# A bucketed attention and expert kernel: a reordered start, pairs 0 and 1 hashed singly, loads behind a gate

## The chip, the cores and the metric

The kernel runs on one core of a Trainium2 chip. The metric is the device time of one execution in microseconds (us). The median of three runs of the kernel before is 390.04 us (389.36 to 390.91).

The engines are TensorE (PE; PEld is its weight load), VectorE (DVE), ScalarE (ACT), GpSimd (POOL) and SyncE (SP). SP and ACT also issue DMAs from their queues.

## What is computed

Attention over 4 batches of 8 heads, 768 tokens, 64 columns, in which a query sees only the keys of its own hash bucket; then one expert layer on the 128 best scored tokens of each batch.

```python
q_bits = (q @ proj > 0); k_bits = (k @ proj > 0)          # 6 bits
mask = bucket(q_bits)[:, None] == bucket(k_bits)[None, :]
scores = where(mask, scale * q @ k.T, -1e9)
attn = softmax(scores) ; o = attn @ v
# per batch: x = o of all heads (768 x 512)
s = x @ w_gate ; top = 128 largest of s
h = max(x[top] @ w1, 0) ; y = h @ w2
out = x ; out[top] += sigmoid(s[top]) * y
```

## The kernel before, in words

Every value that matters is split into a high 16-bit part and a low remainder, so that PE multiplies 16-bit numbers. Heads come in pairs: pair p holds heads 2p+1 and 2p+2 in the two halves of the 128 partitions; head 0 is loaded apart (`init_first`, `load_first`), its operands are split on ACT (`split_first`, `split_second`) and DVE (`low_first`).

For a pair, `load_x` brings the 384 KB of its queries (r = 0) and of its keys (r = 1) on SP's queue. `split_xh` makes the high part in tile T on ACT, `split_xl` the low part on DVE. `k_diff` subtracts the two halves of the keys' high part (GpSimd for pair 0, DVE after). The hash multiplies X by the six projections as 32-bit matmuls into a PSUM bank: `hash_half(g, e)` takes half e of the tokens of the two pairs 2g and 2g+1 together. `signs(g, e)` compares the result with zero on DVE into tile sg and, after the second half, subtracts the two halves of the signs (GpSimd for group 0, DVE after). Head h's operand A is then put together in SBUF by DMAs on SP's queue: `place_a` (the high parts), `place_signs` (the bits, two DMAs), `place_b` and `place_l` (the operands of the low-part product).

For every head, six pairs of matmuls (`max_unit`) give each query's bucket scores; `max_relu` (ACT) and `max_red` (DVE) reduce them to a maximum per query. `max_turn`, `max_copy` and `max_row` turn the maxima into a row of A; head 0 does this in two steps by `row_first` (PE and a copy by ACT). Then come the scores (`st_unit`, two matmuls, `st_exp` on ACT), the remainder of the exponentials (`r_chunk`, DVE or GpSimd), and the product with V (`av`). V's 384 KB are loaded by `load_v` on ACT's queue and split by `split_vh` (ACT) and `split_vl` (DVE). `sum_v` to `seed` prepare what the product starts from. `norm` divides.

The PSUM banks for maxima, hash and rows are four, handed out in a fixed turn (`pmax.take`, `pmax.give`). The expert weights come through `load_w`, one resumption of the generator `weights` at a time.

The order in which instructions are issued is written out by hand: `at` numbers the events and the tuple `ORDER` lists them; a negative number resumes a generator (weights, the choice of tokens, the experts, the last batch's `rank_last`). Every engine runs its own instructions in this order. `mine` remembers the last marked DVE instruction, and `turn` makes a GpSimd instruction wait for it. In the start, `keep_warm` puts matmuls on PE whose result is not used.

At the end, `rank_last` ranks the last batch's tokens: `compare` on DVE counts for each token how many come before it, `count` adds the rest by matmuls with a column of ones, and `pick` makes the selection matrix from rank and position, which 48 matmuls (L1177) then multiply.

Of the kernel before, what the change touches and what calls it, by code (L numbers as in the profile page):

```python
# [12 lines left out]
F16 = mybir.dt.float16  # L13
# [37 lines left out]
TURNS = True  # L51
PJW = 69
# [1315 lines left out]
```

## Time and profile before

| | us |
|---|---|
| median of 3 runs | 390.04 |
| the profiled execution | 389.61 |
| its span, first to last instruction | 387.5 |
| PE busy | 374.8 (97%) |
| DVE busy | 345.9 (89%) |
| ACT busy | 313.3 (81%) |
| GpSimd busy | 181.2 (47%) |

Busy time is an engine's time in instructions; matmuls are pipelined and their ends are modelled, so a busy PE is not a PE at its peak. The granted clock is the share of 2.4 GHz that PE was given. Instructions appear with line, engine, operation, the tile written and those read, partitions x elements.

### The profile page before, as it was taken

To read this page: it belongs to the slowest core of one execution; us is meant where nothing else is said; L and a number is where in the kernel's file an instruction comes from. 1 tells how busy PE (TensorE), PEld (TensorE's weight loads), DVE (VectorE), ACT (ScalarE), POOL (GpSimd) and SP (SyncE) were. 2 spreads that over 40 slices of the span, in tenths; PEclk is the share of its full clock that TensorE was granted. 3 is DMA by queue.
4 is the path that set the end of the run, shared out by engine and by line. 5 is a ranking of instruction groups with operands and counts; after the bars stand their busy time and mean duration, and the time that the engine had idled before them with its cause. 6 is when DMAs were issued, how large, how long until landed. Compare 5 with 4: busy or idle time off the path is not lost.

```text
span 387.5 us, 14129 instructions
## 1 busy us (share of the span) xinstructions
PE 374.8 (97%) x5728; PEld 272.6 (70%) x5738; DVE 345.9 (89%) x935; ACT 313.3 (81%) x665; POOL 181.2 (47%) x103
## 2 busy tenths in 40 slices
PE   6889999999999999999999999999999999999995
PEld 4346777677676777687657877667677788778794
DVE  3889999999899989999999999999999999999842
ACT  7899999899998988988588888988988995774210
POOL 8135567474647275655335362545236352630113
PEclk9799999999999999999999999999999999999999
DMA  7568677677776475565855552756463524010301
GB/s 243 148 193 232 172 199 232 169 203 177 223 209 181 100 214 125 140 188 150 208 136 157 135 155 61 217 161 177 100 178 103 113 58 125 6 38 3 110 29 56
DMA packets 26353, 56.37 MB, mean 145 GB/s; under 512 B 4218, under 2 KB 10942, under 8 KB 26288
## 3 DMA queue, kind: packets, MB, share of 16 engines
q1 hardware_dynamic: 15936, 36.92, 36.6%
q10 hardware_dynamic: 9680, 16.45, 13.5%
q0 software_dynamic: 672, 2.10, 1.7%
q8 instruction: 45, 0.74, 0.8%
q14 instruction: 20, 0.16, 0.2%
HBM read 26.58 MB, written 7.35 MB: 88 GB/s over the span
## 4 chain that ended last, share of the span: by engine, by line
PE 78%; issue 7%; ACT 5%; DVE 5%; DMA 2%; POOL 1%; POOLq 0%; SPq 0%; ACTq 0%; DVEq 0%
PE av L776 24%; PE bank L671 14%; PE st L722 14%; PE st L726 14%; PE bank L463 3%; PE bank L995 3%; PE bank L1019 2%; DMA A<-sg 2%; DVE R L757 2%; ACT me L679 1%; ACT P L740 1%; DMA Xa<-in_qk_dram 1%; DVE mj L688 1%; DVE jks L813 1%; PE bank L598 1%
## 5 line engine op out<-in xcount | busy, mean ns | idle before, releaser
L760 POOL TENSOR_TENSOR R<-P 128x1536 f16<-128x1536 f32 x46 | 133.8, 2910 | 134.4 <-DVE V L556 21.1
L776 PEld LDWEIGHTS <-P 128*128 128x128 bf16 x2304 | 125.8, 98 | 26.7 <-issue 1.3
L776 PE MATMUL av<-V,P 128*128 128x65 f16 (+2 forms) x2304 | 133.3, 193 | 0.1
L776 PE MATMUL av<-V,R 128*128 128x65 f16 (+1 forms) x1152 | 126.4, 193 | 0.0
L740 ACT ACTIVATE P<-st 128x512 f32<-128x512 f32 x192 | 111.9, 598 | 17.7 <-PE av L776 9.7
L722 PE MATMUL st<-A 128*128 128x512 f16 (+1 forms) x384 | 119.3, 326 | 1.4 <-ACT P L740 1.2
L726 PE MATMUL st<-B 128*128 128x512 f16 (+1 forms) x384 | 118.6, 326 | 0.7 <-ACT B L432 0.7
L688 DVE CUSTOM_DVE_ANT_0 mj<-bank,me 128x384 bf16<-128x384 f32 x192 | 102.2, 550 | 15.6 <-ACT me L679 7.4
L671 PE MATMUL bank<-A 128*128 128x384 f16 x384 | 108.4, 329 | 3.8 <-DVE A L410 1.0
L776 PEld LDWEIGHTS <-R 128*128 128x128 f16 x1152 | 105.9, 97 | 0.1
L679 ACT ACTIVATE me<-bank 128x384 f32<-128x384 f32 x192 | 92.4, 491 | 14.8 <-PE bank L671 5.7
L757 DVE TENSOR_TENSOR R<-P 128x768 f16<-128x768 f32 x100 | 96.8, 987 | 0.4 <-ACT P L740 0.2
L742 ACT ACTIVATE P<-st 128x512 f32<-128x512 f32 x96 | 56.9, 596 | 2.2 <-PE st L726 0.7
L671 PEld LDWEIGHTS <-A 128*128 128x128 f16 x384 | 34.8, 98 | 23.1 <-issue 4.8
L726 PEld LDWEIGHTS <-B 128*128 128x128 f16 x384 | 37.5, 98 | 18.0 <-issue 2.5
L722 PEld LDWEIGHTS <-A 128*128 128x128 f16 x384 | 37.4, 97 | 15.8 <-issue 2.5
L502 DVE SCALAR_TENSOR_TENSOR T<-X,T 128x768 f16<-128x768 f32 x32 | 31.4, 992 | 0.0
L495 ACT ACTIVATE T<-X 128x768 f16<-128x768 f32 x32 | 26.6, 841 | 0.4 <-DMA B<-T 0.4
L837 POOL TENSOR_TENSOR w1l<-W,w1h 128x512 bf16<-128x512 f32 x8 | 12.8, 1604 | 13.6 <-DVE M L688 4.9
L837 POOL TENSOR_TENSOR w2l<-W,w2h 128x512 bf16<-128x512 f32 x8 | 12.3, 1545 | 12.5 <-DVE R L757 4.0
L798 DVE TENSOR_TENSOR x<-av,rc 128x384 f32<-128x384 f32 x32 | 17.7, 553 | 0.2
L995 PEld LDWEIGHTS <-w1h 128*128 128x128 f16 x256 | 15.9, 98 | 2.1
(137 smaller groups left out, 409.5 us busy)
## 6 DMA issues: line engine op xcount, KB each, us to landing
X<-in_qk_dram SPq DMA_DIRECT2D x32, 384.0 KB
B<-T SPq DMA_DIRECT2D x62, 192.0 KB
A<-T SPq DMA_DIRECT2D x31, 240.0 KB
V<-in_v_dram ACTq DMA_DIRECT2D x16, 384.0 KB
out_dram<-x ACTq DMA_DIRECT2D x6, 768.0 KB
W<-in_w_dram ACTq DMA_DIRECT2D x8, 512.0 KB
sbc<-scores SPq DMA_DIRECT2D x3, 384.0 KB
A<-sg SPq DMA_DIRECT2D x31, 31.5 KB
```

Of the source, the lines that this page charges most:

```text
L502: mine(nc.vector.scalar_tensor_tensor(t[:, o : o + S], st["X", p, r], XS, t[:, i : i + S], op0=ALU.mult, op1=ALU.subtract))
L671: nc.tensor.matmul(pt[:, :384], a[0][:, t * P : (t + 1) * P], a[1][:, 384:768] if i else K[h % NA], start=True, stop=True,)
L679: nc.scalar.activation(me, st["mx", h, t, 0][:, :384], AF.Relu)
L688: nc.vector.tensor_tensor_reduce(out=jk, in0=st["mx", h, t, 1][:, :384], in1=st["me", h, t], op0=ALU.add, op1=ALU.max, scale=1.0 / MS, sca ...
L722: nc.tensor.matmul(pt[:, o : o + n], a[1][:, c * P : (c + 1) * P], a[0][:, q0 : q0 + n], start=True, stop=False,)
L726: nc.tensor.matmul(pt[:, o : o + n], bt[:, 0, c * P : (c + 1) * P], bt[:, 1, q0 : q0 + n], start=False, stop=True,)
L740: nc.scalar.activation(pp[:, r, 0:512], pt, AF.Exp, scale=ES)
L742: nc.scalar.activation(pp[:, :, 512:768], pt.rearrange("p (a b) -> p a b", a=2), AF.Exp, scale=ES)
L757: mine(nc.vector.tensor_tensor(t[:, r], pp[:, r], hi_view(pp, r), op=ALU.subtract))
L760: turn(nc.gpsimd.tensor_tensor(t, pp, hi_view(pp, a), op=ALU.subtract))
L776: nc.tensor.matmul(o[:, t, :n], l, vv[:, c, hh, v0 : v0 + n], start=False, stop=last and l is lo, skip_group_check=True,)
L995: nc.tensor.matmul(hp[:, f * P : (f + 1) * P], w[:, k, o : o + P], x[:, k * P : (k + 1) * P], start=(f == 0 and k == 0 and i == order[0]), ...
```

## The change

- *Loads.* Of the constants only the identity is loaded early (`load_ident`); the rest of the constants, pair 1's X and V of pair 0 wait for the last of head 0's sign compares on DVE (`gate`). V of pair 0 is issued on SP's queue and no more on ACT's. The issue of V of pair 1 and of the first expert weight stands, on ACT, behind the first two maxima of head 1.
- *Hash.* Pairs 0 and 1 are hashed one at a time, all tokens together (`hash_pair`, `sign_pair`): per pair 64 partitions, two compares, one subtraction, all on DVE.
- *High parts.* `split_xh(0, 1)` and `split_xh(1, 0)` run on GpSimd.
- *Identity.* Its 16-bit copy is made by DVE.
- *The last rank.* A 32-bit matmul with the identity (`behind`) starts the bank of counts with each token's constant, so that the selection compares with the rank alone.
- One score instruction of batch 1 (`HOLD`) becomes a mark for `turn`.
- *Order.* The first 300 or so events are reordered; after that 11 events move by a few places. After `begin` the old order read: `load_x(0,1)`, `load_x(1,0)`, `load_x(1,1)`, four signs of head 0, ..., `load_x(0,0)`, two `max_relu`, ..., `load_first(0)`, ..., `load_v(0)`, `load_consts`, `split_xh(1,0)`, `(1,1)`, `(0,0)`, `make_ident`, ..., `hash_half(0,0)`, `(0,1)`, ..., `k_diff`, `place_a(1)`, ..., `signs(0,0)`, `(0,1)`, ..., `place_signs(1)`, ..., `row_first(1)`, `max_unit(1,4,0)`. The new one reads:

```
load_first(0), sign_first(0,0), init_rest, init_a(1), load_x(0,1), split_xh(0,1), sign_first(1,0),
sign_first(1,1), diff_first, max_unit(0,1,1), max_unit(0,0,0), split_second(0), load_x(0,0),
low_first(0), sign_first(0,1), load_ident, make_ident, max_unit(0,0,1), init_m, max_relu(0,0),
max_red(0,0), max_unit(0,1,0), hash_pair(0), max_relu(0,1), split_xh(0,0), max_red(0,1),
max_unit(0,2,0), max_unit(0,3,0), sign_pair(0), max_unit(0,2,1), load_first(1), split_second(1),
max_relu(0,2), max_relu(0,3), max_unit(0,3,1), max_red(0,2), k_diff(0), load_v(0), max_unit(0,4,0),
max_red(0,3), load_x(1,1), split_vh(0), split_vl(0), load_x(1,0), max_relu(0,4), max_unit(0,5,0),
max_relu(0,5), max_unit(0,4,1), place_a(1), row_first(0), max_unit(0,5,1), sum_v(0), load_consts,
max_red(0,4), split_xh(1,1), st_unit(0,3), st_exp(0,3), max_red(0,5), init_a(2), row_first(1),
st_unit(0,4), sum_hi(0), place_signs(1), max_unit(1,0,0), st_exp(0,4), max_unit(1,4,0),
max_relu(1,0), hash_pair(1), split_xl(0,1), max_relu(1,4), weights(1), split_xl(0,0), load_v(1), ...
```

`keep_warm(2)` and `keep_warm(3)`, eight matmuls each, stand before among head 0's maxima, after in head 1's maxima and in head 2's scores.

```diff
+HOLD = ((1, 1, 4),)
+    def load_ident():
+        nc.sync.dma_start(cs[:, :P], cst[:, :P])
+
     def load_consts():
-        nc.sync.dma_start(cs, cst)
+        behind_of(nc.sync.dma_start(cs[:, P:], cst[:, P:]), "gate", "load")
     def make_ident():
-        nc.scalar.copy(ident16, ident)
+        nc.vector.tensor_copy(ident16, ident)
+    def behind_of(i, key, why):
+        if key in st:
+            tc.add_manual_dep(
+                getattr(i, "ins", i), getattr(st[key], "ins", st[key]).name,
+                mybir.DependencyInfo(mybir.DependencyClass.Sync, mybir.DependencyReason.SCHED_ONLY),
+                reason=why,
+            )
     def load_x(p, r):
-        nc.sync.dma_start(x, qk[p, r])
+        i = nc.sync.dma_start(x, qk[p, r])
+        if p == 1:
+            behind_of(i, "gate", "load")
     def load_v(pr):
-        (nc.scalar if ACT_V else nc.sync).dma_start(t, v[pr])
+        i = (nc.scalar if pr else nc.sync).dma_start(t, v[pr])
+        if not pr:
+            behind_of(i, "gate", "load")
...
         if r:
-            nc.vector.tensor_scalar(
+            st["gate"] = nc.vector.tensor_scalar(
...
+    def hash_pair(p):
+        hp = st["hpp", p] = pmax.take(f"hpp{p}")
+        for e in range(2):
+            for r in range(2):
+                i = 64 * e + 32 * r
+                nc.tensor.matmul(
+                    hp[i : i + 32, :384], pjt[:, 0:32], st["X", p, r][:, e * 384 : (e + 1) * 384],
+                    start=True, stop=True, tile_position=(0, i),
+                )
+
+    def sign_pair(p):
...
+        w = slice(64 * p, 64 * p + 64)
+        hp, t = st["hpp", p], st["sg", 0][w]
+        sd, sg = t[:, : S // 2], t[:, S // 2 :]
+        for e in range(2):
+            i = slice(64 * e, 64 * e + 64)
+            nc.vector.tensor_scalar(
+                sg[:, e * 384 : (e + 1) * 384], hp[i, :384], pjt[i, 66:67], pjt[i, 67:68],
+                op0=ALU.is_gt, op1=ALU.mult,
+            )
+        pmax.give(f"hpp{p}")
+        mine(nc.vector.tensor_tensor(sd, sg[:, 0:384], sg[:, 384:768], op=ALU.subtract))
     def split_xh(p, r):
-        nc.scalar.activation(st["T", p][:, o : o + S], st["X", p, r], AF.Copy, scale=XS)
+        if (p, r) not in {(0,1),(1,0)}:
+            nc.scalar.activation(st["T", p][:, o : o + S], st["X", p, r], AF.Copy, scale=XS)
+        else:
+            nc.gpsimd.tensor_scalar(st["T", p][:, o : o + S], st["X", p, r], XS, None, op0=ALU.mult)
+            if (b, part, t) in HOLD:
+                mine(i)
+    def behind(rp):
+        nc.tensor.matmul(
+            rp[:, :NC], ident, cs[:, 3 * P + NC : 3 * P + 2 * NC], start=True, stop=False, skip_group_check=True
+        )
...
         for t in range(NC):
-            pick(sel, t, rank)
+            nc.vector.tensor_scalar(sel[:, t], iota16, rank[:, t : t + 1], None, op0=ALU.is_equal)
```

## Rows read from the trace of the kernel before

**Rows 1.** The page: busy us (share of span) and instructions of each engine.
```profile
PE 374.8 (97%) x5728; PEld 272.6 (70%) x5738; DVE 345.9 (89%) x935; ACT 313.3 (81%) x665; POOL 181.2 (47%) x103
```

**Rows 2.** Windows: length, busy PE, PEld, DVE, ACT, POOL, granted clock, DMA share, GB/s.
```profile
5.00:10.00 5.00, 3.32 (x23) 1.31 (x23) 2.99 (x5) 4.62 (x8) 4.63 (x18) 0.79 1.03 342
10.00:15.00 5.00, 5.00 (x33) 1.92 (x32) 3.67 (x11) 4.10 (x8) 0.44 (x1) 0.53 0.59 149
15.00:20.00 5.00, 3.57 (x25) 1.56 (x23) 5.00 (x10) 4.39 (x9) 0.91 (x1) 1.00 0.54 152
20.00:25.00 5.00, 3.96 (x34) 2.12 (x32) 4.07 (x14) 4.47 (x11) 2.04 (x1) 1.00 0.96 279
25.00:30.00 5.00, 4.73 (x68) 2.99 (x57) 4.67 (x13) 5.00 (x13) 1.98 (x3) 1.00 0.40 86
```

**Rows 3.** Timeline, 10 to 20.1 us: start, length, engine, line, operation, count [idle before <-releaser].
```profile
10.29 0.35 ACTq L383 DMA_DIRECT2D V<-in_v_dram  x1
...
10.69 2.31 ACT L495 ACTIVATE T<-X 128x768 f16<-128x768 f32 x3
...
11.42 2.78 PE L463 MATMUL bank<-X,pjt 128*32 128x384 f32 x16
...
12.90 0.28 ACT L348 CAST ident<-cs 128x128 f16<-128x128 f32 x1
...
13.31 0.67 DVE L480 TENSOR_SCALAR sg<-bank,pjt 128x384 f16<-128x384 f32 x1
...
15.03 0.91 POOL L489 TENSOR_TENSOR sg<-sg 128x384 f16<-128x384 f16 x1 [4.59 <-DVE sg L480]
...
15.97 1.77 SPq L509 DMA_DIRECT2D A<-sg  x2
...
19.14 0.65 PE L671 MATMUL bank<-A 128*128 128x384 f16 x3 [0.22 <-DMA A<-sg]
19.44 0.34 ACT L454 CAST A<-bank 1x256 f16<-1x256 f32 x1
...
20.05 0.33 PE L671 MATMUL bank<-A 128*128 128x384 f16 x1
```

**Rows 4.** Timeline, 5 to 9 us: head 0's signs and the first X copy.
```profile
5.76 0.57 ACT L415 ACTIVATE s<-bank,pjt 14x384 f32<-14x384 f32 x1
...
5.91 1.39 DVE L410 TENSOR_SCALAR A<-bank,pjt 14x384 f16<-14x384 f32 x2
6.36 0.61 ACT L416 ACTIVATE A<-s,pjt 14x384 f16<-14x384 f32 x1
...
8.12 0.83 ACT L495 ACTIVATE T<-X 128x768 f16<-128x768 f32 x1
```

**Rows 5.** Groups by form, 0 to 36 us: count | busy us, mean ns.
```profile
L679 ACT ACTIVATE me<-bank 128x384 f32<-128x384 f32 x21 | 9.8, 491 | 1.8 <-PE bank L671 0.6 <-PE st L726 0.5 <-DVE M L688 0.4
...
L661 DVE TENSOR_TENSOR T<-T 128x384 f16<-128x384 f16 x2 | 0.8, 378 | 0.0
```

**Rows 6.** Groups by form, 0 to 36 us: GpSimd's memsets and the weights' remainder.
```profile
L321 POOL MEMSET A<- 32x960 f32 x7 | 6.3, 897 | 2.0 <-PE st L722 1.8
...
L837 POOL TENSOR_TENSOR w1l<-W,w1h 128x512 bf16<-128x512 f32 x2 | 2.8, 1406 | 3.0 <-DVE R L757 1.8 <-DMA A<-sg 1.2
```

**Rows 7.** Timeline, 4 to 16 us: head 0's two low parts on DVE.
```profile
4.92 0.95 DVE L438 SCALAR_TENSOR_TENSOR B<-Xa,A 64x768 f16<-64x768 f32 x1 [3.02 <-ACT A L392]
...
15.34 1.41 DVE L438 SCALAR_TENSOR_TENSOR B<-Xa,B 64x768 f16<-64x768 f32 x1
```

**Rows 8.** Timeline, 361 to 372 us: the last rank and selection.
```profile
361.67 1.56 PE L1143 MATMUL bp<-cs,sc 128*128 128x128 f32 x12
...
367.89 1.43 DVE L874 TENSOR_SCALAR sel<-iota,cs,rank 128x128 f16<-128x128 f16 x6
...
368.79 2.84 PE L1177 MATMUL bank<-sel,xs 128*128 128x128 f16 x48
```

**Rows 9.** Timeline of PE, 39 to 42 us: the second group's hash.
```profile
39.83 1.50 PE L463 MATMUL bank<-X,pjt 128*32 128x384 f32 x16
```

More of the change, by code (lines that the diff above doesn't have):

```diff
@@ L360, in mine @@
         st["port"] = i
-    def turn(i):
-        if TURNS and "port" in st:
-            tc.add_manual_dep(
-                getattr(i, "ins", i), getattr(st["port"], "ins", st["port"]).name,
-                mybir.DependencyInfo(mybir.DependencyClass.Sync, mybir.DependencyReason.SCHED_ONLY),
-                reason="port",
-            )
+    def behind_of(i, key, why):
[5 more added lines that the diff above has]
+            )
+    def turn(i):
+        if TURNS:
+            behind_of(i, "port", "port")
     def need(*keys):
@@ L456, in row_first @@
         st[("row1", 0) if e else ("row", 0)] = True
+    def hash_pair(p):
[8 more added lines that the diff above has]
+    def sign_pair(p):
+        if ("sg", 0) not in st:
+            st["sg", 0] = sb.tile([P, S // 2 + S], F16, tag="sg", name="sg0", bufs=2)
+        w = slice(64 * p, 64 * p + 64)
[7 more added lines that the diff above has]
+            )
+            st["sgd", p, e] = True
+        pmax.give(f"hpp{p}")
+        mine(nc.vector.tensor_tensor(sd, sg[:, 0:384], sg[:, 384:768], op=ALU.subtract))
     def hash_half(g, e):
@@ L485, in signs @@
         if e:
-            if g:
-                mine(nc.vector.tensor_tensor(sd, sg[:, 0:384], sg[:, 384:768], op=ALU.subtract))
-            else:
-                nc.gpsimd.tensor_tensor(sd, sg[:, 0:384], sg[:, 384:768], op=ALU.subtract)
+            mine(nc.vector.tensor_tensor(sd, sg[:, 0:384], sg[:, 384:768], op=ALU.subtract))
     def split_xh(p, r):
@@ L812, in score @@
             jk = sb.tile([P, 384], BF16, tag="jks", name=f"jks{b}_{part}_{t}", bufs=2)
-            nc.vector.tensor_tensor_reduce(
+            i = nc.vector.tensor_tensor_reduce(
                 out=jk[:, : d1 - d0], in0=x[:, t, d0:d1], in1=wgt[:, d0:d1],
@@ L862, in compare, with count @@
         ))
-    def count(i, cm, rp):
+    def behind(rp):
+        nc.tensor.matmul(
+            rp[:, :NC], ident, cs[:, 3 * P + NC : 3 * P + 2 * NC], start=True, stop=False, skip_group_check=True
+        )
+    def count(i, cm, rp, first=True):
         for j in range(i, NC):
             nc.tensor.matmul(
-                rp[:, j : j + 1], cm[:, j], oneb[:, 0:1], start=(i == j == NC - 1), stop=(i == 0),
+                rp[:, j : j + 1], cm[:, j], oneb[:, 0:1], start=first and i == j == NC - 1, stop=(i == 0),
                 skip_group_check=True,
@@ L1153, in rank_last @@
         rp = st_bank(f"rp{b}")
+        behind(rp)
         yield
@@ L1161, in rank_last @@
             if i < NC - 1:
-                count(i + 1, cms[i + 1], rp)
+                count(i + 1, cms[i + 1], rp, False)
                 yield
-        count(0, cms[0], rp)
+        count(0, cms[0], rp, False)
         yield
@@ L1242, in body @@
         at(keep_warm, 2 + i, n)
-    for g in range(NH // 4):
+    for p in range(2):
+        at(hash_pair, p)
+        at(sign_pair, p)
+    for g in range(1, NH // 4):
         for e in range(2):
@@ L1246, in body @@
             at(signs, g, e)
+    at(load_ident)
     for fn in (score_v, score_vh, score_vl):
```

308 rows, old and new, of the table ORDER are left out of this document.

## The prediction

> **What bounds the kernel now.** I read three views, in this order. The page's busy shares come first: TensorE (PE) is busy 97% of the span [rows 1], and a busy PE is not a PE at its peak. So a gain must come from a place where PE waits or runs slowly. The windows of the first 30 us show one [rows 2]: from 5 to 10 us PE works 3.32 of 5 us, from 10 to 15 us it is busy all the time but at a granted 0.53 of the clock (mostly the lower level, 1.2 GHz), from 15 to 25 us it works 7.53 of 10. From 25 us on PE (4.73), ACT (5.00) and DVE (4.67) are full together. The start is a chain of small steps, not a rate: head 0's bits and maxima, its row of maxima, then head 1's operands. The timeline of the start is the third view, and what the reader should look for there is what stands in these queues that this chain does not need. There is much of it. ACT makes three copies of X in one stretch of 2.31 us between two maxima; PE runs the hash of pairs 0 and 1 together for 2.78 us; only then can DVE compare (0.67 each), GpSimd subtract (0.91) and SP send head 1's bits (1.77 us of issue), and head 1's first maxima start at 19.14 with that DMA as their releaser [rows 3]. Head 0's second row of maxima is copied at 19.44, ending at 19.78 [rows 3]. These two times, 19.14 and 19.78, are my milestones.
>
> **The change part by part.** Head 0's bits are as before: the same two ACT steps of 0.57 and 0.61 per half and two DVE compares in 1.39, ending at 7.30 [rows 4].
>
> *ACT up to the second row copy.* After the change ACT has, from 5.76 on: four sign steps 2.36; two copies of the second operand, one X copy (0,0), one V copy and the X copy (1,1), each about 0.77 (a third of the 2.31 in [rows 3]; widths are 768 columns), 3.85; six maxima of 0.49 [rows 5], 2.94; the row copies 0.56 (estimate: 512 columns by the 0.34 for 256 in [rows 3] and the 0.49 for 384 in [rows 5]) and 0.34; one exponential, about 0.6 (same estimate). The sum is 10.65, so the row is done at 5.76 + 10.65 = 16.4 if ACT never waits, against 19.78: 3.4 us earlier. What has left the stretch: X copies (0,1) and (1,0), now GpSimd's, and (2,1), put later, 2.3 together; the identity's cast 0.28 and the issue of V's load 0.35 [rows 3]; the rest are waits for maxima that come late.
>
> *Head 1's bits.* The first pair is now hashed alone, behind head 0's first maximum. That maximum is read by ACT at about 9.4 (two signs, a copy, two signs, one maximum after 5.76), which frees the bank. The hash of one pair is half of 2.78 at the same clock, 1.39, so 10.8; two compares of 0.67 [rows 3], 12.2; the subtraction, now on DVE, 0.38 [rows 5], 12.6; the two issues 1.77, 14.4; landing as before 1.4 us behind the issue (19.14 - 15.97 - 1.77), 15.8. Against 19.14 that is 3.3 us earlier. Both milestones move alike, by about 3.3.
>
> *GpSimd's new copies.* No row shows this operation. Bounds: a memset of 960 columns takes 897 ns and a two-input subtraction of 512 columns 1406 ns [rows 6], so 768 columns cost between 0.7 and 2.1 us. I take 1.3, nearer to the memset since one tensor is read, not two. It costs nothing: pair 0's half is on GpSimd once X has landed (before 8.12, when ACT's first copy of it ran [rows 4]), ends by 10.2 even at 2.1, k's subtraction of 0.91 by 11.1, and head 1's large operand goes out about then, ahead of the bits at 12.6. Were this cover gone, the milestone would slip by what exceeds about 1.5 us.
>
> *What DVE takes on.* Two more compares of 0.67 (64 partitions cost as much as 128), two subtractions of 0.38 (one from GpSimd, one because pairs are single), the identity's cast about 0.2: 2.3 us. DVE works 6.66 of the 10 us from 5 to 15 [rows 2], so 3.3 us of idleness hide it; without that cover it would cost up to 2.3.
>
> *A shared port.* One DVE step with two tensors took 0.95 beside a memset and 1.41 beside GpSimd's subtraction [rows 7], 0.46 more. The Trainium skill, "GPSIMD Engine Reference", section 1, says GpSimd shares its SBUF interfaces with VectorE and contends with instructions that have two SBUF inputs; that speaks against more work on GpSimd here, the rows agree, and by it three such steps would cost 1.4 us, 388.6 us in all if nothing covered them. I take zero in the sum, since DVE has the idleness named above.
>
> *Loads behind the gate.* The waits for the last compare at 7.3 stand in SP's queue. Behind them on SP are only V's first load, pair 1's X, the rest of the constants and head 1's operands, none of which is wanted before about 11. V's load moves from ACT's queue to SP's. The gain of the gate itself, a quicker first X, I put at zero; what it may cost is a rival.
>
> *How much survives.* From about event 330 the order is the same as before except for single swaps, so what is gained when PE, ACT and DVE become full stays. The lower bound is what ACT is rid of for good: two copies 1.54, cast 0.28, issue 0.35, 2.2 us. The upper bound is the milestones' 3.3. I take 3.0, nearer to the milestones, because what bounds the rest is PE, which gains the earlier start and not ACT's relief.
>
> *The tail.* The rank's seed adds one 32-bit matmul of 6 columns with its weights. Six of 128 columns took 1.56 us [rows 8], so at most 0.26, at least 0 (in the shade of a DVE wait); I take 0.15, since PE runs without a pause there. The six selections in 1.43 us become simpler, but the 48 matmuls that read them start only after the expert's matmuls and then run at 59 ns each (2.84 / 48) [rows 8], so a faster selection is worth 0. The one new port mark of batch 1's score and the single swaps in the middle: 0, with 0.3 either way.
>
> The sum: -3.0 + 0.15 = -2.85. The profiled execution took 389.61 (span 387.5 and 2.1 around it), 0.43 under the median of 390.04; it becomes 386.76, and the median **387.2**.
>
> **The rivals.** *PE stays at half clock (1.2 GHz).* Before, the granted clock is 0.79, 0.53 and then 1.00 (2.4 GHz) in the three stretches from 5 to 20 us: it rose after one in which PE was busy 5.00 of 5 with the joint hash, maxima and warm-up matmuls [rows 2]. The same 16 hash matmuls take 2.78 at half clock and 1.50 at full [rows 3, 9]. The change takes the dense stretch away: the hash is halved and 16 warm-up matmuls go far behind. The Trainium skill, "TensorE: Matmul & The Clock Gate", Part 1, says the throttled state is the default and activity releases it; by that rule sparser matmuls may delay the release, and the windows bear it out. The price from rows: doubling PE's work from 15 to 20 us needs 3.57 more where 1.43 is idle, 2.1 net; from 20 to 25, 3.96 less 1.04, 2.9; from 25 to 30, 4.73 less 0.27, 4.5 [rows 2]. Busy time overlaps (three maxima in 0.65, one alone 0.33 [rows 3]), so I count six tenths. Half clock to 18 us costs 0.8: **388.0**. *The same, long:* half clock to 28 us costs 0.6 x (2.1 + 2.9 + 2.7) = 4.6, **391.8**, which is slower than before; it decides from about 24 us on, where it eats the 2.85. Against it: at half clock PE becomes the full engine by 15 us, and being full is what preceded the rise.
>
> *Gated loads come late.* Three loads of 0.39 MB start at 7.3. At the 342 GB/s of 5 to 10 us they land by about 12, at the 150 of 10 to 20 us [rows 2] by about 16.5; then pair 1's hash and head 2's bits slip 1 to 2 us. Taking 1.5: **388.7**. For it: the place of pair 1's X behind V. Against: 150 was demand and not capacity.
>
> *Nothing carries on.* The early gain is eaten by the work put off (the X copy of pair 2, DVE's 2.3 us) where ACT and DVE are full, or the gates order nothing that was late: **390.0**.
>
> **How the numbers follow.** The forecast 0.60, the short half clock 0.15, late loads 0.12, nothing 0.06, the long half clock 0.07. The range of the forecast alone: 3.3 and another 0.7 for the spread of the runs (389.36 to 390.91) on the low side, 385.6; 2.2 with 0.3 for the swaps on the high side, 388.5. Of the other cases the short half clock, late loads with their 2 us and a little more belong inside, so the high end is 389.6; outside stay nothing, the long half clock and parts of the others, under 0.2. About 0.5% (1.95 us) is what a measurement can tell from no change. Faster by more: 0.56 of the forecast's 0.60, 0.07 of the short half clock, 0.03 of late loads, 0.66. Slower by more: only the long half clock and mishaps with it, 0.07. Between: 0.27.
>
> **What would show it.** Right: head 0's second row copy near 16.4 instead of 19.78, head 1's first maxima near 15.8 instead of 19.14, and from there every stage about 3 us earlier to the end. GpSimd's copies between 0.7 and 2.1 us with nobody waiting for them. Wrong: a granted clock near 0.5 beyond 15 us; head 1's maxima released by pair 1's or by GpSimd's work; DVE full before 15 us; a shift that is there at 16 us and gone at 50; or a first X that lands no earlier and a hash that waits for it.

## The result and the profile after

The changed kernel takes 392.84 us in the median of five runs (390.39 to 394.08) against 390.04 of before: a ratio of 1.0058, 95% interval 1.0035 to 1.0081. The forecast was 387.2, between 385.6 and 389.6. The profiled execution took 391.89, its span is 389.9, 2.4 more than before's 387.5. TensorE's share of the span is as before (97%), VectorE's busy time is 5.4 us longer [rows 1], 2.6 of it in one blocked step that is shown below. Busy us, share and instructions on the page of the kernel after:

```profile
PE 377.6 (97%) x5740; PEld 273.1 (70%) x5740; DVE 351.3 (90%) x940; ACT 313.0 (80%) x662; POOL 183.8 (47%) x104
```

The windows of the first 30 us answer to [rows 2]: length, busy time of PE, PEld, DVE, ACT and POOL, granted clock, DMA share, GB/s.

```profile
5.00:10.00 5.00, 3.24 (x24) 1.09 (x20) 4.61 (x9) 4.77 (x9) 3.30 (x5) 0.77 0.87 296
10.00:15.00 5.00, 4.48 (x32) 1.54 (x24) 4.53 (x13) 4.29 (x8) 4.76 (x6) 0.50 0.65 204
15.00:20.00 5.00, 5.00 (x40) 2.18 (x31) 4.15 (x10) 3.75 (x10) 1.64 (x1) 0.71 0.65 122
20.00:25.00 5.00, 4.98 (x33) 2.71 (x32) 4.64 (x16) 4.96 (x13) 2.21 (x1) 1.00 1.03 317
25.00:30.00 5.00, 4.84 (x83) 3.73 (x82) 5.00 (x14) 4.99 (x11) 1.88 (x2) 1.00 0.81 219
```

The granted clock is 0.71 from 15 to 20 us, where before had 1.00: TensorE stayed at 1.2 GHz until 17.9 us. The timeline of the start answers to [rows 3] (GpSimd's two copies, the issue of head 1's bits, head 0's second row copy, head 1's first maxima on TensorE and ScalarE):

```profile
7.01 2.19 POOL L533 TENSOR_SCALAR T<-X 128x768 f16<-128x768 f32 x1 [1.64 <-DMA X<-in_qk_dram]
...
12.72 1.77 SPq L547 DMA_DIRECT2D A<-sg  x2
...
14.24 2.40 POOL L533 TENSOR_SCALAR T<-X 128x768 f16<-128x768 f32 x1
...
16.77 0.34 ACT L466 CAST A<-bank 1x256 f16<-1x256 f32 x1
...
17.10 0.85 PE L709 MATMUL bank<-A 128*128 128x384 f16 x2
...
17.84 0.49 ACT L717 ACTIVATE me<-bank 128x384 f32<-128x384 f32 x1
```

The row copy ends at 17.1 instead of 19.78, and head 1's first maxima start on TensorE at 17.10 instead of 19.14 [rows 3]. So the start did come earlier, by 2.0 to 2.7 us. To follow what becomes of it, one small DVE step per head serves as a milestone: the add ahead of a head's reciprocal (L787 before, L825 after). In before those of heads 1, 23 and 24 (counted from 0) are

```profile
48.80 0.17 DVE L787 TENSOR_TENSOR rc<-av,rc 128x6 f32<-128x6 f32 x1
...
278.66 0.17 DVE L787 TENSOR_TENSOR rc<-av,rc 128x6 f32<-128x6 f32 x1
...
288.15 0.16 DVE L787 TENSOR_TENSOR rc<-av,rc 128x6 f32<-128x6 f32 x1
```

and in after

```profile
48.52 0.17 DVE L825 TENSOR_TENSOR rc<-av,rc 128x6 f32<-128x6 f32 x1
...
278.35 0.17 DVE L825 TENSOR_TENSOR rc<-av,rc 128x6 f32<-128x6 f32 x1
...
290.19 0.16 DVE L825 TENSOR_TENSOR rc<-av,rc 128x6 f32<-128x6 f32 x1
```

Read down: of the early start 0.28 us is left at head 1 and 0.31 at head 23; one head later the kernel is 2.04 behind. There are two losses, one between 18 and 48 us and one between 278 and 290.

The second is one instruction. In before, the last of batch 2's score steps (jks, 0.48 each) started 0.59 us ahead of GpSimd's remainder R:

```profile
286.58 0.48 DVE L813 CUSTOM_DVE_ANT_0 jks<-x,wgt,sc 128x256 bf16<-128x256 f32 x1
...
286.99 0.55 DVE L688 CUSTOM_DVE_ANT_0 mj<-bank,me 128x384 bf16<-128x384 f32 x1
287.17 2.75 POOL L760 TENSOR_TENSOR R<-P 128x1536 f16<-128x1536 f32 x1 [5.71 <-ACT P L740]
```

In after, one reduction of maxima (mj) stands ahead of the score steps instead of behind them, and they come later against R:

```profile
285.34 0.55 DVE L726 CUSTOM_DVE_ANT_0 mj<-bank,me 128x384 bf16<-128x384 f32 x1
...
286.63 3.05 DVE L851 CUSTOM_DVE_ANT_0 jks<-x,wgt,sc 128x256 bf16<-128x256 f32 x1
286.65 2.75 POOL L798 TENSOR_TENSOR R<-P 128x1536 f16<-128x1536 f32 x1 [5.50 <-ACT P L778]
...
290.14 0.32 PE L709 MATMUL bank<-A 128*128 128x384 f16 x1 [1.71 <-DVE W L655]
...
291.12 0.49 ACT L717 ACTIVATE me<-bank 128x384 f32<-128x384 f32 x1 [2.48 <-DVE M L726]
```

The score step takes 3.05 us instead of 0.48: it waits for R's whole 2.75. TensorE then stands 1.71 us and ScalarE 2.48 for what VectorE owes them.

### The profile page after: what moved, and what is told of

Its sections match the earlier page's. It is cut to its first block, busy times and chain, and to the rows that moved or that the text cites. A ratio compares the mean times of both kernels' runs of the same rounds, so it can differ in the third digit from the quotient of the medians.

```text
span 389.9 us, 14156 instructions
## 1 busy us (share of the span) xinstructions
PE 377.6 (97%) x5740; PEld 273.1 (70%) x5740; DVE 351.3 (90%) x940; ACT 313.0 (80%) x662; POOL 183.8 (47%) x104
## 4 chain that ended last, share of the span: by engine, by line
PE 76%; DVE 8%; issue 6%; ACT 4%; DMA 3%; POOL 1%; SPq 0%; POOLq 0%; DVEq 0%; ACTq 0%
PE av L814 23%; PE bank L709 15%; PE st L760 14%; PE st L764 14%; PE bank L1040 3%; DMA A<-sg 3%; DVE R L795 2%; DVE jks L851 2%; PE bank L1064 2%; PE bank L501 2%; ACT P L778 1%; ACT me L717 1%; DVE mj L726 1%; DMA Xa<-in_qk_dram 1%; PE bank L636 1%
## 5 line engine op out<-in xcount | busy, mean ns | idle before, releaser
L726 DVE CUSTOM_DVE_ANT_0 mj<-bank,me 128x384 bf16<-128x384 f32 x192 | 102.4, 551 | 10.3 <-PE bank L709 4.8
L709 PEld LDWEIGHTS <-A 128*128 128x128 f16 x384 | 35.2, 98 | 24.5 <-issue 7.0
L531 ACT ACTIVATE T<-X 128x768 f16<-128x768 f32 x30 | 25.1, 841 | 0.4 <-DMA B<-T 0.4
L877 POOL TENSOR_TENSOR w1l<-W,w1h 128x512 bf16<-128x512 f32 x8 | 11.7, 1467 | 18.8 <-DVE T L699 6.5
```

The source lines that it names most:

```text
L709: nc.tensor.matmul(pt[:, :384], a[0][:, t * P : (t + 1) * P], a[1][:, 384:768] if i else K[h % NA], start=True, stop=True,)
L726: nc.vector.tensor_tensor_reduce(out=jk, in0=st["mx", h, t, 1][:, :384], in1=st["me", h, t], op0=ALU.add, op1=ALU.max, scale=1.0 / MS, sca ...
```

## The experiments

Ratios are to before on the same chip, with 95% intervals; where microseconds are worked out from two ratios of different batches, they are 390 times the difference. The order is given by the names of the events; in the code ORDER holds their numbers.

**First question: the collision, the front or the tail?** Three theories stood against each other: that the collision is the whole loss, that the new front is slower by itself, and that the tail's added matmul costs. e1 undoes the one swap at batch 2's score:

```diff
+ choose2 (scores 3 to 5 of batch 2's second part)
  max_red(27, 2)
- choose2
```

> The changed kernel with one step put back: the second step of choose(2) (three scores on DVE) stands again ahead of the reduction max_red(27,2), as before. Theory A (collision): of the loss, 2.2 us come from one score on DVE that took 3.05 us instead of 0.42 at 286.63, because GpSimd's remainder began at 286.65; with the old order DVE is then in a reduction that reads PSUM, the score keeps its 0.42, and the time is 2 to 2.5 us under the changed kernel's 392.84, about 390.4. Theory B (the new front is slower by itself and this place only shows it): another wait takes over, 392 to 393. Theory C (the end of the kernel, with its added matmul): no change, 392 to 393.

Measured: 390.27 us, 1.0017 (1.0006 to 1.0027). In its profile R starts 0.50 behind the last score step, which takes 0.48. By the ratios that is 1.6 us better than after.

e2 leaves the order and marks the step, so that GpSimd waits for it:

```diff
- HOLD = ((1, 1, 4),)
+ HOLD = ((1, 1, 4), (2, 1, 5))
```

> The changed kernel with its order, but the last score of that step (batch 2, part 1, column 5) gets the mark that GpSimd's remainder waits for. Theory A: GpSimd starts about 0.4 us later, behind the score, the score takes 0.42 us, and the time is about 390.4 as in e1_swap_back, 0.2 more at most. Theories B and C: 392 to 393.

Measured: 390.74, 1.0020 (1.0008 to 1.0032); batch 2's three score steps take 0.47 each, and R starts 0.65 behind the last. Two different cures give the same 1.5 to 1.6 us, and both intervals lie under after's (1.0035 to 1.0081): the collision is shown. Both kernels are still not faster than before, so it isn't all.

e3 takes the front alone (after's first 300 events and their code, before's order behind them, no mark, no seeded rank); e4 takes the rest alone.

```diff
  # e3
- ORDER = after
+ ORDER = after[:300] + before[299:]
- HOLD = ((1, 1, 4),)
+ HOLD = ()
```

> The new front alone (loads, single hashes, GpSimd copies, the first 300 events); the order behind it, the scores' marks and the last rank are those of before. Theory A: 0.1 to 0.6 us under before (the shift of head 23's reciprocal in the profiles was 0.4), 389.5 to 390. Theory B: 2 to 3 us over before, 392 to 393. Theory C: as before, 390.

Measured: 389.40, 0.9985 (0.9969 to 1.0002), and a second time, as e3_again:

> The new front with the rest of before, a second time, as the base of the next three runs. It gave 389.40 beside 389.89 of before. Expected 389.2 to 389.7 beside a before of 389.9. Its profiled front ran at the lower clock to 19.4 us; if that end moves from run to run, the theory of the clock (below) expects the times of this kernel to spread by over 1.5 us, as they did the first time (387.96 to 390.70).

Measured: 389.57, 0.9991 (0.9976 to 1.0006), between 388.22 and 391.58. The front is worth about 0.5 us of the 3.0 forecast, and both intervals still hold no gain at all.

> The other half: the front of before with everything behind the first 300 events as in the changed kernel (swaps, the score's mark, the last rank). Theory A: the swapped score meets GpSimd's remainder here too, 2 to 2.8 us over before, 392 to 393. Theory B: as before, 390. Theory C: 392 to 393, but with the loss behind 360 us and not at 286.

Measured: 390.99, 1.0024 (1.0013 to 1.0034): 0.9 us lost. Its profile doesn't show the collision although it has the swap: the last score step has a lead of 0.11 us on R, keeps its 0.48, and R takes 2.97 instead of 2.75. In after the lead is 0.02 and the score step loses. Leads of 0.07 to 0.17 stand in ten other profiles (0.11 in before itself, at batch 1's score), and the score step keeps its 0.48 or 0.49 in all of them. The swap turned a lead of 0.59 into 0.11 and 0.02 in these two profiles; that some executions of after escape, which would explain their wide spread, is argued from this and not shown.

**Second question: where do 2 us of the front go?** Three cures on e3. f1 puts the two groups of eight warm-up matmuls back among head 0's maxima, f2 issues head 3's bits where SyncE's queue is empty, f3 does both.

```diff
  # f1                              # f2
  max_unit(0, 0, 1)                 load_x(3, 1)
+ keep_warm(3, 8)                 + place_signs(3)
  ...                               ...
  max_unit(0, 2, 1)                 max_row(1)
+ keep_warm(2, 8)                   ...
  ...                             - place_signs(3)
- keep_warm(2, 8)   (at 23 us in e3_again)
  ...
- keep_warm(3, 8)   (at 43 us in e3_again)
```

> The kernel e3 with the two groups of eight warm-up matmuls put back among head 0's maxima, one behind its second and one behind its sixth product, where TensorE waits for a bank. Theory 'clock': the front lost its gain because TensorE stays at 1.2 GHz to 17.7 to 19.4 us instead of 14.7; then the clock is full by about 15 us here, the reciprocal of heads 2 to 5 comes 0.5 to 1.5 us earlier than in e3, and the time is about 388.6. Theory 'head 3's bits' and theory 'full engines' (what the front gains has to be given back where TensorE, ScalarE and VectorE are all full): within 0.3 us of e3, whatever the clock does.

> The kernel e3 with the two transfers of head 3's bits issued right behind the load of pair 3's second operand, where SyncE's queue stands empty for 5 us, instead of behind head 1's row of maxima. Theory 'head 3's bits': in after and in e3 these transfers are the last thing that head 3's first maxima wait for (issued 27.7, landed 32.5 in after; in before issued 21.3); then the first maxima of head 3 come 2 us earlier than in e3, the reciprocal of heads 2 to 5 0.8 to 2 us earlier, and the time is about 388.2. Theories 'clock' and 'full engines': head 3's first maxima move, the reciprocals do not, and the time is within 0.3 us of e3.

> Both changes on e3. If clock and bits are two separate losses, the gains of the two add up, about 387.6, faster than before by 0.5%. If the front's gain must be given back to full engines, 389.1 to 389.7 as e3.

Measured: f1 389.15, 0.9976 (0.9964 to 0.9987); f2 389.14, 0.9969 (0.9954 to 0.9983); f3 388.56, 0.9959 (0.9946 to 0.9973). A second time, as f3_again:

> f3 a second time, as the base of the next run and because it is the fastest kernel so far. It gave 0.9959 of before; expected 0.995 to 0.997, 388.3 to 389.0 beside a before of 390.0.

Measured: 388.44, 0.9969 (0.9954 to 0.9984). Against e3_again, on the same chip, f1 is 0.6 us faster, f2 0.9 and f3 1.2; the intervals of f1 and f2 overlap with e3_again's, that of f3's first run just clears it. f3 beats before by 1.2 to 1.6 us and after by 3.5 to 3.9. But the theories failed in their detail. In f1 and f3 the clock is full from 11.4 and 5.6 us on, and head 1's first maximum comes at 18.55 and 18.03, no earlier than in e3_again (18.02). The other profiles say the same: it comes at 17.4 to 18.7 in the ten with a full clock from 13.7 us or earlier, and at 17.8 to 19.0 in the six with half clock to 17.5 us or later. The clock isn't what holds it. In f3 (issue of the bits, TensorE's first maxima of head 1):

```profile
13.00 1.77 SPq L547 DMA_DIRECT2D A<-sg  x2
...
17.67 0.48 PE L709 MATMUL bank<-A 128*128 128x384 f16 x2 [1.02 <-DMA A<-sg]
```

the maxima wait for head 1's bits, 4.67 us after the issue began; in before it was 3.17 (19.14 less 15.97 [rows 3]). And head 3's first maxima come no earlier in f2 than in e3_again (33.42 and 33.26 on ScalarE); what moved is the second reciprocal.

What the cures do is seen in one window, from head 1's first maximum on ScalarE to the second reciprocal's add: length, busy time of PE, PEld, DVE, ACT, POOL, clock, DMA share, GB/s. Before:

```profile
19.91:48.80 28.89, 27.50 (x383) 18.28 (x382) 26.10 (x71) 28.01 (x63) 15.24 (x8) 1.00 0.72 199
```

After:

```profile
17.84:48.52 30.68, 29.64 (x397) 19.64 (x397) 28.39 (x73) 28.15 (x62) 13.88 (x8) 1.00 0.73 200
```

The window is 1.79 us longer: TensorE has 2.14 us more to do in it and stands 0.35 less. The early start was partly bought by putting work behind the milestone: pair 1's hash (0.85), sixteen warm-up matmuls, and for VectorE two compares, a subtraction and a low part (2.3). One profile is not much here: the same window is 28.86 to 28.89 us in all four kernels with before's front (before, e4, h2, h3), but 30.28 to 31.47 in the five with after's (after, e1, e2, e3 twice). That it is longer with the new front is sure, how much is not. e3_again and the cured kernels f1, f2 and f3 in this order:

```profile
18.02:49.11 31.09, 29.43 (x396) 19.45 (x389) 28.50 (x73) 28.01 (x62) 13.87 (x8) 1.00 0.69 199
```

```profile
18.55:49.24 30.69, 28.98 (x381) 18.70 (x381) 28.84 (x75) 27.99 (x61) 13.62 (x8) 1.00 0.70 198
```

```profile
18.17:48.43 30.26, 29.62 (x397) 19.63 (x397) 28.47 (x74) 28.30 (x62) 13.88 (x8) 1.00 0.72 208
```

```profile
18.03:47.92 29.89, 28.97 (x381) 18.77 (x381) 28.27 (x74) 28.08 (x61) 13.82 (x8) 1.00 0.71 207
```

Against e3_again f1 has 0.45 us less work for TensorE and a window 0.40 shorter, which is within that spread; in f2 TensorE's idleness falls from 1.66 to 0.64 and the window by 0.83, to just under the spread; f3's is 1.20 shorter, and f3_again's (29.90) agrees.

A window is TensorE's work and its idleness together, whatever the cause; more is learned from where the idleness stands. With after's front much of it stands in one place, ahead of head 2's scores. Before (the copy of head 2's row of maxima, and head 2's first scores):

```profile
34.24 0.25 ACT L703 CAST mr<-bank 6x128 f16<-6x128 f32 x1 [0.22 <-PE bank L698]
...
38.28 0.38 PE L722 MATMUL st<-A 128*128 128x512 f16 x1
```

After:

```profile
35.03 0.24 ACT L741 CAST mr<-bank 6x128 f16<-6x128 f32 x1
...
38.54 0.39 PE L760 MATMUL st<-A 128*128 128x512 f16 x1 [0.67 <-ACT T L531]
```

These scores in e3_again, then in f3:

```profile
39.13 0.39 PE L760 MATMUL st<-A 128*128 128x512 f16 x1 [1.50 <-DMA A<-mr]
```

```profile
37.99 0.39 PE L760 MATMUL st<-A 128*128 128x512 f16 x1 [0.26 <-DMA A<-mr]
```

In after head 0's first scores start 1.47 us earlier than in before (15.20 for 16.67) and head 1's 1.21 earlier (28.48 for 29.69), but head 2's row of maxima is copied 0.79 later, and its scores start 0.26 later. The early start is lost there. TensorE doesn't wait in before; with after's front it waits 0.34 to 1.60 us, for the transfer of the row in four of the five profiles; in f2 0.41, in f3 0.26. What is shorter in f2 and f3 is that transfer: its issue starts at 35.05 in e3_again, 35.21 in f2 and 35.15 in f3, and the scores that need it at 39.13, 38.20 and 37.99.

**Third question: which engine bounds that window?** On f3, useless work of 1.9 us for VectorE (g1), 1.7 for ScalarE (g2), 16 more hash matmuls for TensorE (g3), all at 18 to 20 us; and GpSimd's two remainders of head 1 in before's order (g4).

```diff
  # g1, g2: in sign_pair(1), behind the subtraction
+ for k in range(2):
+     nc.vector.scalar_tensor_tensor(dz, X, XS, T, mult, subtract)   # g1
+     nc.scalar.activation(dz, X, Copy, scale=XS)                    # g2
  # g3: in hash_pair(1)
+ for k in range(3):
      nc.tensor.matmul(hp, ...)
  # g4
- r_chunk(1, 0)
  r_chunk(1, 4)
+ r_chunk(1, 0)
```

> The kernel f3 (the new front with clock and bits cured) with 1.9 us of useless work for VectorE at about 20 us, behind pair 1's subtraction: two more steps of the kind that makes an operand's low part (0.95 each), into a tile that nobody reads. It asks which engine the stretch from 18 to 48 us is bound by. Theory 'VectorE is full': VectorE worked 44.5 us up to the second reciprocal of before (at 48.8) and 47.4 to 47.6 in after and f3 (at 48.5 and 47.9), so the 3 us that the change gave it left it no idleness; then the second reciprocal comes 1.3 to 1.9 us later than in f3 and the time is about 390.0. Theory of the prediction, 'TensorE bounds it and VectorE has idleness to hide 2.3 us': under 0.5 us later, 388.6 to 389.0.

> The same with 1.66 us of useless work for ScalarE at the same place (two more copies of X, 0.83 each). If VectorE alone is full, under 0.5 us later than f3 (388.6 to 389.0); if ScalarE too is full in this stretch (it is busy 24 of the 25 us from 25 to 50 in f3), 1.2 to 1.7 us later, about 389.9.

> The same with 1.5 us of useless work for TensorE at the same place (pair 1's eight hash matmuls run three times over). If TensorE is what bounds the stretch, as predicted, 1 to 1.5 us later than f3, about 389.8; if VectorE is, under 0.6 us (the compares of pair 1 wait for it, nothing else).

> f3 with GpSimd's two remainders of head 1 in before's order (the pair of chunks 4 and 5 ahead of 0 and 1). In after and f3 chunk 0's comes first, and head 1's first products, which read chunk 4, wait for the second remainder until 39.0 us (TensorE busy 4.33 and 4.52 of the 5 us from 35 to 40, against 5.00 in before). If that wait is a loss, the reciprocals come 0.3 to 0.7 us earlier than in f3, about 388.1; if ScalarE or VectorE is what is late there, no change (388.4 to 388.8).

Measured: g1 390.30, 1.0000 (0.9987 to 1.0012); g2 390.18, 0.9997 (0.9984 to 1.0010); g3 391.84, 1.0041 (1.0026 to 1.0055); g4 388.96, 0.9971 (0.9958 to 0.9985). Against f3's 0.9959 the doses cost 1.6, 1.5 and 3.2 us (0.4 less each against f3_again's 0.9969). g1's profile has a disturbance of its own: from 20 to 24.5 us TensorE was busy 2.59 of 4.50, and then the granted clock was 0.50 until 27.92, so part of this dose may have been paid through the clock. (The busy times in g1's theory are too high: up to the second reciprocal VectorE works 38.7 us in before and 41.6 to 41.7 in f3 and after, so it had idleness left.) g3's dose was larger than meant:

```profile
18.66 4.15 PE L476 MATMUL bank<-X,pjt 128*32 128x384 f32 x24
```

24 matmuls take 4.15 us where eight take 0.85, so the dose was 3.3, not 1.5, and came back almost whole. g4 gains nothing; the wait for the second remainder, though the chain of waits in f3 runs through it, wasn't a loss. Since most of every dose came back, the doses don't single out an engine. Taking work away was meant to. h1 leaves out pair 1's compares and subtraction on VectorE, h4 two of ScalarE's copies, h5 both; GpSimd writes zeros there.

```diff
  # h1, in sign_pair(1)
- two compares, one subtraction (DVE)
+ nc.gpsimd.memset(t, 0)
  # h4, in split_xh(2, 1) and split_vh(1)
- nc.scalar.activation(hi, x, Copy, scale)
+ nc.gpsimd.memset(hi, 0)
```

> f3 with VectorE's work on pair 1's bits left out (two compares of 0.68 and a subtraction of 0.35, 1.7 us, at 19 to 20.6 us); GpSimd, idle there, writes zeros in their place, so heads 3 and 4 get wrong bits and all other work stays. If the work that the change gave VectorE is what ate the front's gain, the second reciprocal comes 1.0 to 1.7 us earlier than in f3 and the time is about 387.2 (0.992 of before). If what is full is ScalarE or TensorE, under 0.5 us earlier (388.1 to 388.9).

> f3 with two of ScalarE's copies between 26 and 30 us left out (the high parts of pair 2's second operand and of V of pair 1, 0.83 each, 1.7 us); GpSimd writes zeros there, so their heads come out wrong and all other work stays. ScalarE is busy 14.7 of the 15 us from 20 to 35 in f3. If ScalarE is what the front's gain is lost to, the second reciprocal comes 1.0 to 1.6 us earlier than in f3 (which had -0.9 against before, so about -2.2) and the time is about 387.2. If ScalarE and VectorE are both full, so that taking from one uncovers the other, under 0.6 us, as when VectorE was relieved (second reciprocal -1.46).

> f3 with both reliefs: ScalarE's 1.7 us and VectorE's 1.7 us left out, GpSimd writing zeros in both places. If either engine covers for the other, this one gains what neither relief gained alone: the second reciprocal 1.2 us or more earlier than in f3, about 387.0. If neither matters because the chain of TensorE and the transfers sets the time, -0.5 at most, as with VectorE alone.

Measured: h1 389.38, 0.9990 (0.9976 to 1.0005); h4 389.07, 0.9983 (0.9971 to 0.9994); h5 388.85, 0.9977 (0.9962 to 0.9992). None is faster than f3. The same window, h1, h4 and h5:

```profile
17.67:47.34 29.67, 28.47 (x381) 18.71 (x381) 27.26 (x72) 27.77 (x61) 13.64 (x8) 1.00 0.72 205
```

```profile
18.49:48.86 30.37, 29.03 (x381) 18.69 (x381) 28.85 (x73) 26.99 (x59) 15.52 (x10) 1.00 0.73 204
```

```profile
18.12:48.26 30.14, 28.80 (x381) 18.71 (x381) 27.25 (x70) 26.91 (x59) 15.52 (x10) 1.00 0.71 205
```

VectorE or ScalarE or both have 1.0 to 1.2 us less to do (and GpSimd 1.7 more in h4 and h5), and the window changes by -0.2, +0.5 and +0.2; TensorE's work stays at 28.5 to 29.0. So my theory of that stage, that VectorE's new work ate the gain, isn't borne out.

The doses and reliefs missed the place, though. The add ahead of head 0's reciprocal, in before, after and f3:

```profile
37.30 0.17 DVE L787 TENSOR_TENSOR rc<-av,rc 128x6 f32<-128x6 f32 x1
```

```profile
34.71 0.17 DVE L825 TENSOR_TENSOR rc<-av,rc 128x6 f32<-128x6 f32 x1
```

```profile
34.73 0.17 DVE L825 TENSOR_TENSOR rc<-av,rc 128x6 f32<-128x6 f32 x1
```

From it to head 1's add pass 11.50 us in all four profiles with before's front, 13.48 to 14.63 in the five with after's, and 13.18 to 13.29 in all nine of f3 and what was built on it (f3 twice, g1 to g4, h1, h4, h5). What g1 to g3, h1, h4 and h5 added or took away ahead of head 0's add shifted that add and changed nothing in the stretch behind it. In before TensorE and ScalarE work without a pause from the one add to the other; in f3 TensorE works 12.71 of the 13.19. Four matmuls and two reductions of head 3's maxima and a low part on VectorE stand in this stretch that stood ahead of head 0's add before, so part of the 2.6 us by which head 0 is early is only their being put off. Which steps of the new order cost the 1.7 us that f3 keeps, no run singles out, and it stays open.

**Fourth question: what does the rest cost besides the collision?** h2 is e4 without the mark on batch 1's score; h3 is before with the mark, the seeded rank and the changed selection, in before's order.

```diff
  # h2 (on e4)
- HOLD = ((1, 1, 4),)
+ HOLD = ()
```

> The kernel e4 (before's front, after's order of all that follows) without the port mark on batch 1's score (1,1,4). In e4 the reciprocals fell back by 0.45 us between heads 15 and 17 (196 to 209 us), where the mark stands, and by 0.4 at head 22. If the mark makes the first step, it is gone here and the time is about 390.5 beside 391.0 of e4; if the single swaps make it, the step stays at 0.4 to 0.5.

> Before with everything of the change that is not its front and not its order: the port mark, the rank's seed by a matmul, the changed selection. If the single swaps cost the 0.9 us that e4 lost, this is before plus the tail's 0.17: 389.9 to 390.5 beside 390.1, reciprocals within 0.1 us of before's up to the last. If the mark costs, a step of 0.4 at head 16 shows.

Measured: h2 394.33, 1.0137 (1.0113 to 1.0160); h3 390.28, 1.0016 (1.0004 to 1.0028). I had taken the mark for a cost. It is the cure of a second collision; in h2:

```profile
206.38 0.48 DVE L814 CUSTOM_DVE_ANT_0 jks<-x,wgt,sc 128x256 bf16<-128x256 f32 x1
206.45 3.02 POOL L761 TENSOR_TENSOR R<-P 128x1536 f16<-128x1536 f32 x1 [2.86 <-ACT P L741]
206.79 0.08 DVE L814 DVE_READ_ACCUMULATOR2_ANT sc<- 128x1 f32 x1
206.79 2.96 DVE L814 CUSTOM_DVE_ANT_0 jks<-x,wgt,sc 128x256 bf16<-128x256 f32 x1
```

With the swaps of the order, batch 1's score also meets R, and without the mark the kernel is 4.4 us slower by the ratios (h2 against e4). The profiles show 2.5 of them at this place: from head 15's reciprocal to head 16's h2 loses 2.9 us against before, e4 0.4. Where the rest arises is not shown; the profiled execution of h2, 392.68, is the fastest of its six. Batch 2's score has the same swap and no mark. Of the 0.9 us that e4 loses, h3's part (mark, seed and selection) is 0.6, hardly above what the runs can tell; the 0.3 left for the swaps is within the noise.

## Why the prediction was wrong, point by point

**What bounds the kernel.** The rows of the start were read rightly: the chain of small steps did shorten, but that the stretch behind it is TensorE's is not settled. Relief of ScalarE and VectorE brings nothing (h1, h4, h5) and 2.8 to 3.2 of TensorE's 3.3 us come back (g3); but most of what g1 and g2 gave the other two came back as well.

**ACT up to the row copy, and head 1's bits.** ACT's sum was about right (10.27 us of work from 5.60 to 17.11, forecast 10.65), but ACT also waited 1.2 us, so the row copy ended at 17.1 and not at 16.4. Head 1's bits were issued at 12.72, forecast 12.6. The term behind it was too small: "landing as before 1.4 us behind the issue" is 2.9 in f3 (17.67 less 13.00 and 1.77), where nothing but the transfer is waited for, and in after TensorE, at half clock, came to these maxima only at 17.10. Instead of 3.3 the milestone gained 2.0 to 2.1.

**GpSimd's copies** took 2.19 and 2.40 us, more than the upper bound of 2.1 and far from the 1.3 chosen. Nobody waited for them directly in after or f3; but behind the first of them GpSimd clears the tile M, and VectorE's first reduction waits 0.23 us for that, which in f3 lies on the chain to head 1's bits.

**The clock.** The rival of the short half clock is what happened (to 17.9 us), but its price of 0.8 us is not found at the milestone: with the clock full from 5.6 us on, f3's is no earlier. In the medians f1 and f3, which put the warm-up matmuls back, are 0.4 to 0.6 us faster than e3_again and f2, with intervals that overlap; what of this is the clock and what the sixteen matmuls behind the milestone, no run tells. The two profiles of e3 are a caution: the clock rose at 19.4 us in the first and 17.5 in the second, and the second reciprocal came 1.4 later in the first, 0.5 of which stood already at head 0's first maximum.

**The gated loads** were not late: in after neither pair 1's X nor V of pair 0 is waited for. (The landing times in that rival are off: three loads of 0.39 MB from 7.3 us land at 10.7 by the one rate and 15.2 by the other, not 12 and 16.5.)

**How much survives.** This is the first failed step. I took 3.0 because "from about event 330 the order is the same", and asked what was removed ahead of the milestone, not what was put behind it. 2.14 us of TensorE's work and 2.29 of VectorE's went there. Of 2.07 us 0.28 survived to head 1's reciprocal in after's profile; in the other four profiles with this front (e1, e2, e3 twice) nothing did, that reciprocal came 0.24 to 1.70 us later than in before. Of e3 as a whole about 0.5 us survived in the medians. The loss stands at head 2's row of maxima, which came no earlier than before, as shown above; that the work put behind the milestone is the reason fits this and is argued, since no run takes it away.

**VectorE's 2.3 us** were sized well, and called hidden, rightly as it seems: leaving out 1.7 of them gained nothing.

**The swaps and the mark, "0, with 0.3 either way".** This is the second failed step and carries the sign: a swap of two DVE steps cost 2.35 us in the profile (from 0.31 ahead at head 23 to 2.04 behind at head 24), 1.6 in the medians. I had weighed the shared port for the new front only and counted the DVE steps' durations, not their lead on GpSimd's remainder. The Trainium skill, "SBUF — State Buffer", section "Who interferes with whom", says that a DVE instruction with two SBUF inputs contends with a GpSimd instruction that reads SBUF, that the shared ports are an exclusive lock, and that the order of issue decides who blocks. The trace agrees on who contends: the score step, which reads x and the gate's weights, took 3.05 beside a remainder of 2.75, while the reduction mj, which reads one tile from PSUM and one from SBUF, took its 0.55 beside before's remainder (287.17). On the order it agrees only with a margin, since the score step that lost has the earlier record, by 0.02. By that section the swap should have been a rival of its own.

**The tail** cost 0.2, as forecast (0.15): from the last reciprocal's add to the end it is 27.5 us against 27.3.

The sum, in the one profile of after: 2.07 earlier at the milestone, 1.79 given back behind it, 2.35 for the collision, 0.2 for the tail, and 0.1 in between make the 2.4 of the span. (The low end of the range, 385.6, was counted from the profiled 389.61; from the median, as the forecast was, it is 386.0.)

## What to carry to other kernels

An earlier milestone is only a gain if the next ones come earlier too: add up, for the engine that is full, what a reordering puts behind the milestone, and follow the shift from head to head before calling it kept (here it was there at head 1's scores and gone at head 2's). A dose or a relief tells about the stretch that it falls into and no other. Where two engines share a port, a swap of neighbours may not be free: look for the lead that one has on the other, and call a lead of some tenths of a microsecond a risk of the whole longer instruction, in the steady part of the kernel as much as where the change is meant to act. Where a mark holds one such place, look at the others of its kind.

## What had not been expected of the hardware

- A lead decides 2.6 us: with 0.59, 0.50, 0.11 and 0.07 us the DVE step kept its 0.48, with 0.02 it took 3.05 although its record starts first; with R already 0.34 under way it took 2.96.
- A product with a constant of 128x768 32-bit numbers into 16 bits takes GpSimd 2.13 to 2.40 us (29 of 32 in the profiles here; the others up to 2.90), against 1.41 of its two-input subtraction of 128x512 and 0.90 of a memset of 32x960 [rows 6].
- 32-bit matmuls of 384 columns took 4.15 us for 24 records, 173 ns each, where six in a row went to the same 32 rows of a bank (g3); eight records, two in a row to each of four groups of rows, took 0.85, 106 each (f3). Why is not shown.
- The same program's TensorE clock became full at different times in two profiles: 5.6 and 10.3 us in f3, with the milestone at 18.03 and 17.93, and 19.4 and 17.5 us in e3, with 19.03 and 18.02.
